# Layernorm pipelined over tiles, and the first scale block applied where the transposes leave PSUM

## The chip, the cores and the metric

The kernel runs on one core of one Trainium2 chip. The time is the device time of one execution in microseconds (us), given as a median of several executions. A core has these engines: PE (TensorE, matrix products), DVE (VectorE), ACT (ScalarE), POOL (GpSimd) and SP (SyncE, which here only issues transfers). PE reads SBUF, the large on-chip memory, and writes PSUM, a small one of eight banks, from which DVE or ACT must fetch the results. Each engine works through its own instructions in order.

## The reference

It is the attention half of a two-stream diffusion block: image tokens and text tokens are normalised and modulated by a conditioning vector `c`, projected, attend to each other jointly, and go through a gated output projection with a residual. B = 2, 256 image and 32 text tokens per batch element, D = 1152, all in bf16.

```python
mod_i = (silu(c) @ wmod_img).reshape(B, 6, 1, D)     # likewise mod_t with wmod_txt
shi, sci, gai = mod_i[:, 0], mod_i[:, 1], mod_i[:, 2]
hi = layernorm(x_img) * (1 + sci) + shi              # likewise ht
qkvi = hi @ wqkv_img                                 # likewise qkvt
q, k, v = concatenated text and image parts of qkvt, qkvi
p = softmax(q @ k.T * D ** -0.5)
a = p @ v
out_i = x_img + gai * (a_img @ wo_img)               # likewise out_t
```

## The kernel before, in words

The order of work is written out by hand: the pools are under a manual schedule, so every engine executes its instructions in the order of the program text, and waits between engines come from the data and from buffers.

The 512 image tokens are four tiles of 128 (`NIT` = 4, two for each batch element). D = 1152 is nine blocks of 128 (`KT` = 9). SP loads the tiles of x and then, block group by block group, the columns of the scale part of `wmod_img` (`w_sc_i`) and the matching rows of the V part of `wqkv_img` (`w_v_i`). The groups are `KC`, in the kernel before (0,2), (2,4), (4,6), (6,9). After them come the text tokens, the shift weights `w_sh_i`, the Q weights `w_q_i` in three pieces, and the other weights through six rotating buffers (`wpool`).

The image part begins like this:

- `silu_c` turns `c` to columns with a PE transpose and computes silu with an exponential on ACT (L124) and three DVE operations; the result is `sT`.
- `ln_stats` (L143 to L147) takes three `bn_stats` and one `bn_aggr` on DVE and the square root on ACT. `ln_apply` (L151, L152) takes the reciprocal and normalises on DVE.
- `x_transposes` (L161, L162) turns a normalised tile into nine 128x128 blocks, five in one PSUM buffer `tp` and four in another, and ACT copies them to `hT_i`.
- `mod_scale` (L169, L177, L179) computes 1 + scale for the blocks of one group: nine matmuls with a two-column right side for each block, and then one write to `mod_img`, on ACT or DVE.
- `apply_mod` (L187, L192, L196) multiplies blocks of `hT_i` by the scale in place, on DVE, POOL or ACT.
- `v_part` (L208) adds the blocks of one group to the V sums of one tile and one half of 512 columns. There are seven such sums (`va`), open from the first group to the last, and the buffers of PSUM for them and for `tp` are the seven of the pool `ps_mm`.

The program text interleaves these: while tiles 2 and 3 are normalised and transposed, the V matmuls of the second group run for tiles 0 and 1 already. When all groups are through, `v_rest` (L296) computes the last 128 columns of V, then come the shift (L308 to L312) and Q (L373). After that come K, the text stream, softmax, attention and the output projection (L560), which the change leaves alone.

Of the kernel before, what the change touches and what calls it, by code (L numbers as in the profile page):

```python
# [8 lines left out]
ACT = mybir.ActivationFunctionType  # L9
ALU = mybir.AluOpType  # L10
# [4 lines left out]
def kernel(  # L15
# [14 lines left out]
    nc = tc.nc  # L30
    bf = mybir.dt.bfloat16
    f32 = mybir.dt.float32
    PSUM = bass.MemoryType.PSUM

    B, NI, D = x_img.shape
    NT = x_txt.shape[1]
    P = 128
    KT = D // P
    NTOK = NI + NT
    NIT = (B * NI) // P  # L40
    TPB = NI // P
    NTT = B * NT
    CH = 384
    NCH = D // CH
# [1 line left out]
    SCALE = float(D) ** -0.5  # L46
    EPS = 1e-5

    KC = [(0, 2), (2, 4), (4, 6), (6, KT)]
    VW = 512  # L50
    NM = 1024

    const = ctx.enter_context(tc.tile_pool(name="const", bufs=1))
    wpool = ctx.enter_context(tc.tile_pool(name="w", bufs=6))
    act = ctx.enter_context(tc.tile_pool(name="act", bufs=1))
    work = ctx.enter_context(tc.tile_pool(name="work", bufs=2))
    small = ctx.enter_context(tc.tile_pool(name="small", bufs=4))
    ps_mm = ctx.enter_context(tc.tile_pool(name="ps_mm", bufs=7, space=PSUM))
# [11 lines left out]
    def w_view(src):  # L70
        return src.rearrange("(kt p) n -> p kt n", p=P)
# [10 lines left out]
    x_i = act.tile([P, NIT, D], bf)  # L82
    w_sc_i = wpool.tile([P, KT, D], bf, tag="w", name="w_sc_i")
    w_v_i = wpool.tile([P, KT, D], bf, tag="w", name="w_v_i")

    def load_x(i):
        nc.sync.dma_start(x_i[:, i, :], xi_t[:, i, :])

    def load_pair(ch):
        k0, k1 = KC[ch]  # L90
        nc.sync.dma_start(w_sc_i[:, :, k0 * P:k1 * P], w_view(wmod_img)[:, :, D + k0 * P:D + k1 * P])
        nc.sync.dma_start(w_v_i[:, k0:k1, :], w_view(wqkv_img)[:, k0:k1, 2 * D:3 * D])

    load_x(0)
    load_x(1)
    load_pair(0)
    load_x(2)
    load_x(3)
    for ch in range(1, len(KC)):
        load_pair(ch)  # L100
    x_t = act.tile([NTT, D], bf)
# [3 lines left out]
    w_q_i = load_w(wqkv_img, 0, K3)  # L105


    ident = const.tile([P, P], bf)
    make_identity(nc, ident[:])
    eps_t = const.tile([P, 1], f32)  # L110
# [10 lines left out]
    def silu_c():  # L121
        cT_ps = ps_sm.tile([P, B * KT], bf, tag="sm")
        nc.tensor.transpose(cT_ps[:], c18[:], ident[0:B * KT, 0:B * KT])
        nc.scalar.activation(e18[:], cT_ps[:], ACT.Exp, scale=-1.0)  # L124
        nc.vector.tensor_scalar_add(e18[:], e18[:], 1.0)
        nc.vector.reciprocal(e18[:], e18[:])
        nc.vector.tensor_mul(sT[:], cT_ps[:].rearrange("p (b kt) -> p kt b", b=B),
                             e18[:].rearrange("p (b kt) -> p kt b", b=B))
        nc.gpsimd.tensor_copy(sT32[:, :, 0:B], sT[:])
# [3 lines left out]
    def evac(out_ap, in_ap):  # L133
        if evac_idx[0] % 2 == 0:
            nc.vector.tensor_copy(out_ap, in_ap)  # L135
        else:
            nc.scalar.copy(out_ap, in_ap)  # L137
        evac_idx[0] += 1

    def ln_stats(x_ap, np_):  # L140
        stats = small.tile([P, NCH, 6], f32, tag="stats")
        for k in range(NCH):
            nc.vector.bn_stats(stats[0:np_, k, :], x_ap[:, k * CH:(k + 1) * CH])  # L143
        mv = small.tile([P, 2], f32, tag="mv")
        nc.vector.bn_aggr(mv[0:np_, :], stats[0:np_, :, :])
        rstd = small.tile([P, 1], f32, tag="rstd")
        nc.scalar.activation(rstd[0:np_, :], mv[0:np_, 1:2], ACT.Sqrt, bias=eps_t[0:np_, :])  # L147
        return mv, rstd

    def ln_apply(x_ap, np_, out_ap, mv, rstd):  # L150
        nc.vector.reciprocal(rstd[0:np_, :], rstd[0:np_, :])  # L151
        nc.vector.tensor_scalar(out_ap, x_ap, mv[0:np_, 0:1], rstd[0:np_, :], op0=ALU.subtract, op1=ALU.mult)  # L152

    xn_i = act.tile([P, NIT, D], bf, tag="A")
    hT_i = act.tile([P, KT, B * NI], bf, tag="Bt")

    def x_transposes(i):
        for (k0, k1) in ((0, 5), (5, KT)):
            tp = ps_mm.tile([P, 5, P], bf, tag="mm")
            for kt in range(k0, k1):  # L160
                nc.tensor.transpose(tp[:, kt - k0, :], xn_i[:, i, kt * P:(kt + 1) * P], ident[:])  # L161
            nc.scalar.copy(hT_i[:, k0:k1, i * P:(i + 1) * P], tp[:, 0:k1 - k0, :])  # L162

    mod_i = const.tile([P, 2 * KT, B], f32, name="mod_img")

    def mod_cols(wt, out_ps, j0, j1):
        for j in range(j0, j1):
# [4 lines left out]
    def mod_scale(ch, eng):  # L172
        k0, k1 = KC[ch]
        mps = ps_sm.tile([P, KT, B], f32, tag="sm")
        mod_cols(w_sc_i, mps, k0, k1)
        if eng == "dve":
            nc.vector.tensor_scalar_add(mod_i[:, KT + k0:KT + k1, :], mps[:, 0:k1 - k0, :], 1.0)  # L177
        else:
            nc.scalar.activation(mod_i[:, KT + k0:KT + k1, :], mps[:, 0:k1 - k0, :], ACT.Identity, bias=1.0)  # L179

    def apply_mod(kt, t0, t1, shift, eng):
        b = t0 // TPB
        sl = hT_i[:, kt, t0 * P:t1 * P]
        ap = mod_i[:, kt, b:b + 1] if shift else mod_i[:, KT + kt, b:b + 1]
        op = ALU.add if shift else ALU.mult
        if eng == 0:
            nc.vector.tensor_scalar(sl, sl, ap, None, op0=op)  # L187
        elif eng == 1:
            if shift:
                nc.gpsimd.tensor_scalar(sl, sl, 1.0, ap, op0=ALU.mult, op1=ALU.add)  # L190
            else:
                nc.gpsimd.tensor_scalar(sl, sl, ap, 0.0, op0=ALU.mult, op1=ALU.add)  # L192
        elif shift:
            nc.scalar.activation(sl, sl, ACT.Identity, bias=ap, scale=1.0)
        else:
            nc.scalar.activation(sl, sl, ACT.Identity, scale=ap)  # L196
# [5 lines left out]
    def v_part(i, half, ch):  # L202
        k0, k1 = KC[ch]
        if ch == 0:
            vacc[i, half] = ps_mm.tile([P, VW], f32, tag="mm", name=f"va{i}{half}")
        ps = vacc[i, half]
        for kt in range(k0, k1):
            nc.tensor.matmul(ps[:], lhsT=hT_i[:, kt, i * P:(i + 1) * P], rhs=w_v_i[:, kt, half * VW:(half + 1) * VW],  # L208
                             start=(kt == 0), stop=(kt == KT - 1))
        if k1 == KT:  # L210
            evac(v_i[:, i, half * VW:(half + 1) * VW], ps[:])


    silu_c()
    st = ln_stats(x_i[:, 0, :], P)
    ln_apply(x_i[:, 0, :], P, xn_i[:, 0, :], *st)
    x_transposes(0)
    st = ln_stats(x_i[:, 1, :], P)
    mod_scale(0, "act")
    ln_apply(x_i[:, 1, :], P, xn_i[:, 1, :], *st)  # L220
    for kt in range(*KC[0]):
        apply_mod(kt, 0, 1, False, 1)
    x_transposes(1)
    for half in range(2):
        v_part(0, half, 0)
    st = ln_stats(x_i[:, 2, :], P)
    for kt in range(*KC[0]):
        apply_mod(kt, 1, 2, False, 1)
    ln_apply(x_i[:, 2, :], P, xn_i[:, 2, :], *st)
    mod_scale(1, "act")  # L230
    for half in range(2):
        v_part(1, half, 0)
    for kt in range(*KC[1]):
        apply_mod(kt, 0, 2, False, 1)
    x_transposes(2)
    st = ln_stats(x_i[:, 3, :], P)
    for kt in range(*KC[0]):
        apply_mod(kt, 2, 3, False, 1)
    ln_apply(x_i[:, 3, :], P, xn_i[:, 3, :], *st)
    for i in range(2):  # L240
        for half in range(2):
            v_part(i, half, 1)
    x_transposes(3)
    for half in range(2):
        v_part(2, half, 0)
    for kt in range(*KC[0]):
        apply_mod(kt, 3, 4, False, 1)
    for kt in range(*KC[1]):
        apply_mod(kt, 2, 4, False, 0)
    mod_scale(2, "dve")  # L250
    for n, kt in enumerate(range(*KC[2])):
        apply_mod(kt, 0, 2, False, n % 2)
        apply_mod(kt, 2, 4, False, (n + 1) % 2)
    v_part(3, 0, 0)
    for half in range(2):
        v_part(2, half, 1)
    v_part(3, 0, 1)
    v_i = act.tile([P, NIT, D], bf, tag="A")
    SEVEN = [(i, half) for i in range(NIT) for half in range(2)][:7]
    for (i, half) in SEVEN[:4]:  # L260
        v_part(i, half, 2)
    mod_scale(3, "dve")
    for b in range(B):
        for n, kt in enumerate(range(*KC[3])):
            apply_mod(kt, b * TPB, (b + 1) * TPB, False, (n + b) % 3)
    for (i, half) in SEVEN[4:]:
        v_part(i, half, 2)
    for (i, half) in SEVEN:
        v_part(i, half, 3)


    xn_t = act.tile([NTT, D], bf)
    st_t = ln_stats(x_t[:, :], NTT)
    ln_apply(x_t[:, :], NTT, xn_t[:, :], *st_t)
    junk = small.tile([P, 1], f32, bufs=1)
    nc.scalar.activation(junk[:], eps_t[:], ACT.Exp)

# [129 lines left out]
    for blk, wq in enumerate([w_q_t, w_k_t]):  # L407
        for j0 in range(0, KT, FG):
            jn = min(FG, KT - j0)
            ps = ps_mm.tile([P, FG, NTT], f32, tag="mm")  # L410
            for j in range(j0, j0 + jn):
                for kt in range(KT):
                    nc.tensor.matmul(ps[:, j - j0, :], lhsT=wq[:, kt, j * P:(j + 1) * P], rhs=hT_t[:, kt, :],  # L413
                                     start=(kt == 0), stop=(kt == KT - 1))
# [212 lines left out]
```

## Time and profile before

| What | Value |
|---|---|
| median of 3 runs | 126.28 us (125.22 to 126.29) |
| profiled execution, its own time | 125.21 us |
| span of its instructions | 123.4 us |
| PE, DVE, ACT, POOL busy | 110.2, 54.0, 34.5, 25.2 us |
| transfers | 41.05 MB, mean 333 GB/s |
| granted TensorE clock | 0.998 |
| first scale matmul (L169) | 7.87 us after the span's start |
| transposes of tiles 0 to 3 (L161) start | 6.75, 9.79, 14.15, 16.87 us |
| first matmul of `v_rest` (L296) | 28.94 us |

The span runs from the first to the last instruction; the time of an execution holds some 2 us around it. Busy time is the union of an engine's instructions. "Idle before" and "<-" in rows of the profile name how long an engine stood before an instruction and what ended its wait. The chain of waits follows the work that ended last back from the end, so its rows add up to the span; the timeline merges neighbouring instructions of one form and gives start, length and count.

### The profile page before, as it was taken

The numbers are of one execution on the slowest core, as the hardware profiler recorded it, in microseconds if no ns is written. First come the engines' busy times: TensorE is split into PE (matmuls) and PEld (weight loads), VectorE is DVE, ScalarE is ACT, GpSimd is POOL, SyncE is SP. The second block draws the span as 40 slices with busy tenths as digits, with TensorE's granted clock in tenths as the row PEclk, the third lists the DMA queues.
The fourth block names the chain that finished last, engine by engine and source line by source line (L and its number), as shares of the span: only waits on it lengthen the run. The fifth ranks groups of instructions, "written<-read, shape, count | busy, mean of one in ns | idle before, by whom it ended". The sixth has DMA issues, their size and how long they took to land.

```text
span 123.4 us, 2694 instructions
## 1 busy us (share of the span) xinstructions
PE 110.2 (89%) x1137; PEld 66.8 (54%) x1137; DVE 54.0 (44%) x129; ACT 34.5 (28%) x85; POOL 25.2 (20%) x68
## 2 busy tenths in 40 slices
PE   0058989999999999999999999899969999999990
PEld 0044635546874445445444449767748766656660
DVE  0777633247690222202030621144275656646581
ACT  5444350231680301110031122143775500012000
POOL 4004334391064030304230000005260000000000
PEclk9999999999999999999999999999999999999999
DMA  3999999999999999999999999999999994220222
GB/s 107 270 365 377 376 383 319 353 415 408 415 403 407 403 411 409 412 409 406 406 377 384 404 414 413 404 412 406 408 403 420 373 410 190 90 96 0 101 80 64
DMA packets 22631, 41.05 MB, mean 333 GB/s; under 512 B 1179, under 2 KB 6459, under 8 KB 22619
## 3 DMA queue, kind: packets, MB, share of 16 engines
q1 hardware_dynamic: 21776, 39.74, 85.8%
q0 software_dynamic: 672, 1.06, 2.3%
q8 instruction: 9, 0.15, 0.5%
q10 hardware_dynamic: 171, 0.08, 0.2%
q14 instruction: 3, 0.02, 0.0%
HBM read 39.53 MB, written 1.35 MB: 331 GB/s over the span
## 4 chain that ended last, share of the span: by engine, by line
PE 82%; DVE 7%; ACT 5%; DMA 2%; issue 1%; ACTq 0%
PE qkps L373 29%; PE ps L560 13%; PE va L208 10%; PE aps L498 6%; PE gps L334 5%; PE ps L413 4%; PE sps L438 4%; PE mps L169 3%; ACT hT_i L162 2%; DMA x_i<-in_x_img_dram 2%; PE tp L161 2%; PE ps L579 2%; PE ps L296 2%; PE ps L303 2%; DVE v_t L135 1%; DVE xn_i L152 1%
## 5 line engine op out<-in xcount | busy, mean ns | idle before, releaser
L373 PE MATMUL qkps<-hT_i,t 128*128 128x512 bf16 x162 | 35.7, 379 | 0.0
L373 PEld LDWEIGHTS <-t 128*128 128x128 bf16 x162 | 15.5, 98 | 19.0 <-issue 0.7
L560 PE MATMUL ps<-t,aT 128*128 128x384 bf16 (+2 forms) x117 | 18.1, 314 | 0.0
L208 PE MATMUL va<-w_v_i,hT_i 128*128 128x512 bf16 x63 | 15.9, 401 | 0.1
L560 PEld LDWEIGHTS <-aT 128*128 128x128 bf16 x117 | 11.0, 98 | 6.8 <-issue 0.5
L563 DVE SCALAR_TENSOR_TENSOR tmp<-ps,rs,gb 128x384 bf16<-128x384 f32 (+2 forms) x13 | 7.6, 586 | 7.1 <-PE ps L560 7.1
L357 DVE TENSOR_SCALAR qkT<-qkps 128x512 bf16<-128x512 f32 x5 | 3.5, 692 | 15.4 <-PE qkps L373 15.4
L208 PEld LDWEIGHTS <-hT_i 128*128 128x128 bf16 x63 | 6.1, 102 | 6.9 <-issue 1.5
L192 POOL TENSOR_SCALAR hT_i<-hT_i,mod_img 128x128 bf16<-128x128 bf16 (+1 forms) x14 | 6.1, 450 | 14.5 <-ACT mod_img L179 6.5
L161 PE MATMUL tp<-ident,xn_i 128*128 128x128 bf16 x36 | 3.6, 265 | 5.7 <-DVE xn_i L152 5.7
L498 PE MATMUL aps<-pT,v_i 128*128 128x288 bf16 x36 | 6.7, 286 | 1.2 <-DVE rs L527 1.2
L344 POOL DMA_DIRECT2D mod_scratch<-g_sb x8 | 4.8, 600 | 12.9 <-DVE g_sb L338 6.1
L137 ACT CAST qkT<-qkps 128x512 bf16<-128x512 f32 x5 | 2.8, 586 | 16.0 <-PE qkps L373 16.0
L135 DVE CAST qkT<-qkps 128x512 bf16<-128x512 f32 x4 | 2.8, 688 | 8.4 <-PE qkps L373 8.4
L161 PEld LDWEIGHTS <-xn_i 128*128 128x128 bf16 x36 | 2.8, 120 | 6.6 <-DVE xn_i L152 6.4
L162 ACT COPY hT_i<-tp 128x640 bf16<-128x640 bf16 (+1 forms) x8 | 4.7, 642 | 5.9 <-PE tp L161 5.9
L143 DVE BATCH_NORM_STATS2 stats<-x_i 128x6 f32<-128x384 bf16 x12 | 5.9, 548 | 0.4 <-DMA x_i<-in_x_img_dram 0.4
L359 ACT ACTIVATE qkT<-qkps 128x512 bf16<-128x512 f32 x4 | 2.3, 596 | 11.4 <-PE qkps L373 11.4
L413 PE MATMUL ps<-hT_t,t 128*128 128x64 bf16 x162 | 5.0, 193 | 0.4 <-issue 0.4
L413 PEld LDWEIGHTS <-t 128*128 128x128 bf16 x162 | 4.9, 98 | 0.8 <-issue 0.5
L135 DVE CAST aT<-aps 128x288 bf16<-128x288 f32 x9 | 4.1, 458 | 2.5 <-PE aps L498 2.5
L498 PE MATMUL aps<-pT,v_t 128*128 128x288 bf16 x18 | 5.1, 286 | 0.0
(112 smaller groups left out, 128.9 us busy)
## 6 DMA issues: line engine op xcount, KB each, us to landing
t<-in_wmod_txt_dram SPq DMA_DIRECT2D x3, 2592.0 KB, 22.4
t<-in_wqkv_txt_dram SPq DMA_DIRECT2D x3, 2592.0 KB, 20.1
t<-in_wmod_img_dram SPq DMA_DIRECT2D x2, 2592.0 KB, 18.6
t<-in_wqkv_img_dram SPq DMA_DIRECT2D x6, 864.0 KB, 15.0
t<-in_wo_img_dram SPq DMA_DIRECT2D x1, 2592.0 KB, 22.3
t<-in_wo_txt_dram SPq DMA_DIRECT2D x1, 2592.0 KB, 24.3
w_sc_i<-in_wmod_img_dram SPq DMA_DIRECT2D x3, 576.0 KB, 7.6
w_v_i<-in_wqkv_img_dram SPq DMA_DIRECT2D x3, 576.0 KB, 7.9
```

Source lines behind the costliest of these rows:

```text
L135: nc.vector.tensor_copy(out_ap, in_ap)
L143: nc.vector.bn_stats(stats[0:np_, k, :], x_ap[:, k * CH:(k + 1) * CH])
L161: nc.tensor.transpose(tp[:, kt - k0, :], xn_i[:, i, kt * P:(kt + 1) * P], ident[:])
L162: nc.scalar.copy(hT_i[:, k0:k1, i * P:(i + 1) * P], tp[:, 0:k1 - k0, :])
L192: nc.gpsimd.tensor_scalar(sl, sl, ap, 0.0, op0=ALU.mult, op1=ALU.add)
L208: nc.tensor.matmul(ps[:], lhsT=hT_i[:, kt, i * P:(i + 1) * P], rhs=w_v_i[:, kt, half * VW:(half + 1) * VW], start=(kt == 0), stop=(kt == K ...
L334: nc.tensor.matmul(gps[32 * g:32 * g + 32, :], lhsT=lhs[:, kt, :], rhs=w_blk[:, kt, g * VC:(g + 1) * VC], start=(kt == 0), stop=(kt == KT ...
L373: nc.tensor.matmul(pss[j - j0][:], lhsT=wq[:, kt, j * P:(j + 1) * P], rhs=hT_i[:, kt, :], start=(kt == 0), stop=(kt == KT - 1))
L413: nc.tensor.matmul(ps[:, j - j0, :], lhsT=wq[:, kt, j * P:(j + 1) * P], rhs=hT_t[:, kt, :], start=(kt == 0), stop=(kt == KT - 1))
L498: nc.tensor.matmul(aps[:], lhsT=lhsT, rhs=pT[:, kj, :], start=(kj == 0), stop=(kj == 2))
L560: nc.tensor.matmul(ps[:, 0:cw], lhsT=aT[:, dt, t0:t0 + P], rhs=w_o_i[:, dt, cs], start=(dt == 0), stop=(dt == KT - 1))
L563: nc.vector.scalar_tensor_tensor(tmp[:, 0:cw], ps[:, 0:cw], rsum[(b, qi)][:], gb[:, b, cs], op0=ALU.mult, op1=ALU.mult)
```

## The change

The change touches only the part up to the last V group.

- `KC` becomes three groups of three blocks. SP loads x0, x1, the first scale group, x2, the first V group, x3, and then the pairs of the other two groups.
- A constant tile `junk_in` is set on DVE, and 13 matmuls of 128x512 on it (`keep_busy`) stand on PE: two ahead of the transposes of `c`, eleven behind. Their result is not used.
- Normalising is cut into steps (`Norm`). `norm_step(i)` takes the root of tile i, the first third of the statistics of tile i+1, applies tile i, and takes the other two thirds.
- `mod_scale(0)` comes ahead of everything of tile 0 but its statistics. `x_transposes(i)` moves the first three blocks into a PSUM buffer of their own, and three ACT activations with a per-partition scale write them to `hT_i`, already multiplied. The other six blocks go through a second buffer and one copy. The scaling of the first group by `apply_mod` is gone.
- After a tile's transposes come its V matmuls of the first group. The second and third group begin when all four tiles are through: `mod_scale` with its write on DVE, `apply_mod` shared over DVE, POOL and ACT for three blocks and both batch elements, then all V matmuls of the group.
- The text stream uses the same `Norm`.

```diff
-    KC = [(0, 2), (2, 4), (4, 6), (6, KT)]
+    KC = [(0, 3), (3, 6), (6, KT)]
...
-    load_pair(0)
+    nc.sync.dma_start(w_sc_i[:, :, 0:CH], w_view(wmod_img)[:, :, D:D + CH])
     load_x(2)
+    nc.sync.dma_start(w_v_i[:, 0:3, :], w_view(wqkv_img)[:, 0:3, 2 * D:3 * D])
     load_x(3)
...
+    junk_in = const.tile([P, VW], bf)
+    nc.vector.memset(junk_in[:], 1.0)
...
+    class Norm:
...
+        def part(self, k):
+            nc.vector.bn_stats(self.stats[0:self.n, k, :], self.x[:, k * CH:(k + 1) * CH])
+
+        def root(self):
+            nc.vector.bn_aggr(self.mv[0:self.n, :], self.stats[0:self.n, :, :])
+            nc.scalar.activation(self.rstd[0:self.n, :], self.mv[0:self.n, 1:2], ACT.Sqrt, bias=eps_t[0:self.n, :])
+
+        def apply(self):
+            nc.vector.reciprocal(self.rstd[0:self.n, :], self.rstd[0:self.n, :])
+            nc.vector.tensor_scalar(self.out, self.x, self.mv[0:self.n, 0:1], self.rstd[0:self.n, :],
+                                    op0=ALU.subtract, op1=ALU.mult)
...
     def x_transposes(i):
-        for (k0, k1) in ((0, 5), (5, KT)):
-            tp = ps_mm.tile([P, 5, P], bf, tag="mm")
-            for kt in range(k0, k1):
-                nc.tensor.transpose(tp[:, kt - k0, :], xn_i[:, i, kt * P:(kt + 1) * P], ident[:])
-            nc.scalar.copy(hT_i[:, k0:k1, i * P:(i + 1) * P], tp[:, 0:k1 - k0, :])
+        b = i // TPB
+        k1 = KC[0][1]
+        tp = ps_mm.tile([P, k1, P], bf, tag="mm", name="tpa")
+        for kt in range(k1):
+            nc.tensor.transpose(tp[:, kt, :], xn_i[:, i, kt * P:(kt + 1) * P], ident[:])
+        for kt in range(k1):
+            nc.scalar.activation(hT_i[:, kt, i * P:(i + 1) * P], tp[:, kt, :], ACT.Identity,
+                                 scale=mod_i[:, KT + kt, b:b + 1])
+        tp = ps_mm.tile([P, KT - k1, P], bf, tag="mm", name="tpb")
+        for kt in range(k1, KT):
+            nc.tensor.transpose(tp[:, kt - k1, :], xn_i[:, i, kt * P:(kt + 1) * P], ident[:])
+        nc.scalar.copy(hT_i[:, k1:KT, i * P:(i + 1) * P], tp[:])
...
+    warm = ps_mm.tile([P, VW], f32, tag="mm")
+    def keep_busy(n):
+        for _ in range(n):
+            nc.tensor.matmul(warm[:], lhsT=junk_in[:, 0:P], rhs=junk_in[:], start=True, stop=True)
+    keep_busy(2)
     silu_c()
+    keep_busy(11)
+    norms = [Norm(x_i[:, i, :], P, xn_i[:, i, :]) for i in range(NIT)]
+    for k in range(NCH):
+        norms[0].part(k)
+    def norm_step(i):
+        norms[i].root()
+        if i + 1 < NIT:
+            norms[i + 1].part(0)
+        norms[i].apply()
+        if i + 1 < NIT:
+            norms[i + 1].part(1)
+            norms[i + 1].part(2)
+    def v_tile(i, ch):
+        for half in range(2):
+            if (i, half) != (NIT - 1, 1):
+                v_part(i, half, ch)
+    mod_scale(0, "act")
+    norm_step(0)
     x_transposes(0)
+    v_tile(0, 0)
+    norm_step(1)
     x_transposes(1)
+    v_tile(1, 0)
+    norm_step(2)
     x_transposes(2)
+    v_tile(2, 0)
+    norm_step(3)
     x_transposes(3)
+    v_tile(3, 0)
     v_i = act.tile([P, NIT, D], bf, tag="A")
+    for ch in (1, 2):
+        mod_scale(ch, "dve")
+        for b in range(B):
+            for n, kt in enumerate(range(*KC[ch])):
+                apply_mod(kt, b * TPB, (b + 1) * TPB, False, (n + b) % 3)
+        for i in range(NIT):
+            v_tile(i, ch)
```

The removed hand-written order of tiles, scalings and V groups stands in the listing of the kernel before.

## The prediction

> **What bounds the kernel now.** I read the page first, then the chain of waits in order of time, then the timeline of the first 30 us, where the whole change lies. The page:
>
> ```profile
> span 123.4 us, 2694 instructions
> PE 110.2 (89%) x1137; PEld 66.8 (54%) x1137; DVE 54.0 (44%) x129; ACT 34.5 (28%) x85; POOL 25.2 (20%) x68
> PE 82%; DVE 7%; ACT 5%; DMA 2%; issue 1%; ACTq 0%
> ```
>
> PE is the bound, and the last line says that 18% of the chain is on others. The chain shows where (start, length, what):
>
> ```profile
> 7.50 1.18 ACT hT_i L162 x2
> 8.68 0.20 ACT rstd L147
> 8.90 0.17 DVE rstd L151
> 9.10 0.64 DVE xn_i L152
> 9.79 1.14 PE tp L161 x9
> 10.93 1.71 PE va L208 x4
> ...
> 16.87 0.47 PE tp L161 x5
> 17.34 0.02 issue
> 17.36 0.70 ACT hT_i L162
> 18.06 0.04 issue
> 18.10 0.59 PE va L208 x2
> ...
> 23.26 5.85 PE va L208 x27
> 29.11 1.00 PE ps L296 x18
> ```
>
> Two things are to be seen. The top six lines are a loop: ACT copies tile 0's transposes, only then takes tile 1's root, DVE normalises, PE transposes: tile 0's transposes began at 6.75, so 9.79 - 6.75 = 3.04 us from tile to tile. And at 17.34 to 18.10 PE stands until ACT has emptied a transpose buffer: the seven buffers of ps_mm are all taken. From 18.10 PE is unbroken to about 87 us, so what is lost or won before `v_rest` (L296, first matmul 28.94) shifts the end one for one.
>
> The timeline of the start (start, length, engine, line):
>
> ```profile
> 2.90 1.28 ACT L147 ACT_TABLE_LOAD   x1
> 5.58 0.29 ACT L147 ACTIVATE rstd<-mv,eps_t 128x1 f32<-128x1 f32 x1 [1.40 <-DVE mv L145]
> 7.87 0.56 PEld L169 LDWEIGHTS <-w_sc_i 128*128 128x128 bf16 x18 [0.25 <-DMA w_sc_i<-in_wmod_img_dram]
> 8.76 0.17 ACT L179 ACTIVATE mod_img<-mps 128x4 f32<-128x4 f32 x1
> 23.56 0.91 ACT L196 ACTIVATE hT_i<-hT_i,mod_img 128x256 bf16<-128x256 bf16 x2 [5.02 <-DVE mod_img L177]
> ```
>
> The root's table is loaded at 2.90 under idle time, the root runs at 5.58, and the first scale block, which a transfer releases at 7.87, holds back no normalising.
>
> **The change, part by part.**
>
> *Dummies.* 13 of 128x512. Cold rows (four L208 in 1.71 us) give 0.427 each, 5.6 in all; warm rows (16 in 3.48) 0.216, 2.8 in all. The constant's memset on DVE isn't in the trace: between 0.06 (eps_t, 128x1) and 0.69 (a 128x512 cast of DVE); I take 0.3, under DVE's idle time up to 2.91. Begun near 1.2 the dummies end between 4.5 and 7.5, while PE waits for the scale block anyway: cost 0. If the block came before them, the rest of them (up to 1 us) would be paid.
>
> *Transfers.* SP now sends x0, x1, 384 instead of 256 scale columns, x2, three blocks of V, x3. The scale slice grows from 576 to 864 KB. The extra 0.295 MB, at the 411 GB/s seen later, costs 0.7 us, at the 253 of 4 to 6 us 1.2. The windows of 6 to 10 us moved 326 and 386; I take 0.73, so the first scale matmul starts at 8.60 (ends of the range 8.5 and 9.1). x2, V and x3 follow, 2.0 MB more at about 370 GB/s to some 12.6, each ahead of its use below. Later loads keep their order in bytes.
>
> *What is queued on ACT.* `mod_scale(0)` now stands ahead of `norm_step(0)`. On ACT this puts the write of `mod_img` ahead of the first root, and so the first normalising of x waits for a weight transfer that it doesn't use. Behind that activation stand the table load, root 0, and through them DVE's apply and all transposes; on PE too tile 0's transposes stand behind the scale matmuls. The trace shows each load with the line of the activation that follows it; that the load isn't placed ahead of the `mod_img` write is my reading, worth between 0 and 1.28 us. I take 1.28, since L147's load is listed for the root's line. So: 27 scale matmuls 0.82 (the x27 row at 22.44) to 9.42; write 0.04 + 0.17 to 9.63; load 1.28 to 10.92; root 0.30 to 11.23; reciprocal 0.03 + 0.17; apply 0.03 + 0.58 to 12.05; transposes of tile 0 from 12.10. Now they start at 6.75.
>
> On this load the Trainium skill, "ScalarE: Activation LUTs", section "What ACT_TABLE_LOAD costs", speaks against the change more strongly: it adds a drain of about 1.38 us to each switch. The trace shows a root-side load of 1.28 and, for L124, its activation 10 ns behind the load. By the page the sum would be 1.4 us higher; I go by the row.
>
> *Eviction with the scale.* ACT's 128x128 scaled read isn't in the trace. Nearest rows: the scaled 128x256 (two in 0.91: start to start 0.41) and the root, 128x1 with a pointer (0.30 long, 0.20 start to start). Three of them cost 0.6 to 1.2; midway, 0.30 each, 0.9. The copy of six blocks: L162 takes 592 ns over four blocks and 692 over five, which gives 0.79 over six, of which 0.68 before the next may start. ACT per tile is 0.9 + 0.68 + 0.20 = 1.8 where it was 1.2. Removed in exchange: POOL's scalings of chunk 0 (L192, about 0.36 a block), which now delay the first V matmuls.
>
> *The period from tile to tile.* The root of tile i+1 is still written behind tile i's evictions on ACT. From the end of apply: 0.05 to PE, 0.35 until ACT reads, 0.9, 0.68, root 0.30, reciprocal 0.20, apply 0.61: 3.1 us. DVE's own work hides in it (three statistics 1.48, aggregate 0.24, reciprocal 0.17, apply 0.59 = 2.5). PE's work is 9 x 0.056 + 6 x 0.216 = 1.8, so PE idles 1.3 a tile: now it fills these gaps with V of chunk 1, and the new order has nothing there. Tile 3 is transposed from 12.1 + 3 x 3.1 = 21.4, now at 16.87.
>
> *Tile 3 and the seven buffers.* Six V sums are open then, so `tpa` has the last buffer; `tpb` waits for its three evictions, `va` for the copy of `tpb`. From 21.4: evictions done at 1.4, six transposes and copy to 2.8, three V matmuls to 3.5. With a free buffer it would be 1.5; the bounds of this wait are 0 and 2.0, and the row at 17.36 to 18.10 says that the waiting is real.
>
> *Chunks 1 and 2.* Each begins with 27 scale matmuls (0.85 to the last result) and then needs blocks that aren't scaled: write 0.20, first apply 0.32, and POOL's 0.57 for the second block (0.3 more on PE). Now `mod_scale` runs under V matmuls already released. Each chunk: 0.85 + 0.20 + 0.34 + 0.3 + 20 x 0.216 + 0.02 = 6.03, twice 12.05. `v_rest` starts at 21.4 + 3.5 + 12.05 = 36.95.
>
> *The sum.* 36.95 - 28.94 = 8.0 us later. What follows is the same PE work. Its weights land no later than now, but for those whose buffers come free up to 8 us later; the output weights among them land 8.7 us and more ahead of a use that is 8 us later too, so nothing is added. The profiled execution took 125.21 (span 123.4 and 1.8 around it): 133.2. It lies 1.07 under the median of 126.28; from the median it would be 134.3. I predict 133.8.
>
> *Clock.* Nine transposes take 1.14 us at 9.79 and 0.68 at 16.87, though the granted clock reads 1.00 in both: PE runs at half rate until about 13.5 us, after 3.7 us of unbroken work. The dummies give 3 to 6 us of work, so I expect full rate by 8.6. After them come some 2 us idle, 0.8 of scale work and 2.7 idle; no row shows whether that cools PE. Bounds: no loss; or half rate, where a tile's PE work of 9 x 0.107 + 6 x 0.427 = 3.5 exceeds the period by 0.4. I take no loss.
>
> The Trainium skill, "TensorE: Matmul & The Clock Gate", section "HAM oscillation — how this bites in real kernels", states that idle stretches beyond about 3.4 us bring the slow clock back. Neither stretch is so long alone; by it the sum stands, with half a microsecond to lose if both count as one.
>
> **Rivals.** *The load is hidden* or stands ahead of the `mod_img` write: 1.3 less; with a milder wait for buffers (1.3 less) 130.6. For it: the load waits for no data. Against: program order on ACT.
>
> *PE is cold in the tile stage*, so the dummies don't do what they are for: 0.4 on each of four tiles and half of 3.7 us while it warms up again: 133.2 + 3.5 = 136.7. For it: the two idle stretches. Against: PE is busy 60% of the time after.
>
> *Faster: PE alone sets the pace.* Warm from the first scale block on and fed without a gap, PE needs 81 x 0.025 + 36 x 0.056 + 63 x 0.216 = 17.6 us from 8.6: `v_rest` at 26.2, 2.7 earlier, of which the shift weights (landed at 29.51, needed at about 29.3 then) take 0.2: 122.7. It decides only if a tile's turn through ACT and DVE falls to 1.8 us and the first root isn't held at the scale block. Against it: DVE alone has 2.5 us a tile.
>
> **How the numbers follow.** Forecast 0.70, hidden load 0.12, cold PE 0.12, faster 0.04, and 0.02 for balance near zero. The range of 130.3 to 137.2 runs from the hidden load and mild buffer wait to the cold clock, and leaves out the faster case and the ends. A measurement of this kernel can tell about 1% (1.3 us) from no change; faster by more 0.04, within 0.03, slower 0.93.
>
> **What would show it.** Right: the table load just behind the `mod_img` write near 9.6; transposes of the tiles at about 12.1, 15.2, 18.3 and 21.4; PE waiting for ACT ahead of tile 3's second group of transposes; `v_rest` at about 37. Wrong: the first transposes before 10, tiles less than 2.5 apart, or `v_rest` before 29.

## The result, and the profile after

The changed kernel takes 135.26 us in the median of four runs (134.64 to 136.05), the kernel before 126.26 beside it: a ratio of 1.0753, with a 95% interval of 1.0701 to 1.0805. That is slower, as forecast, 1.5 us above the predicted 133.8 and inside the range. The profiled execution took 136.05 (span 134.3); it is the slowest of its four, and that of the kernel before (125.21) is the fastest of its own, so the profiled times put the loss at 10.8 us where the medians put it at 9.0. Ratios leave out executions that lie more than 1.5% above the fastest of their kernel; medians do not. The page of the changed kernel, with the clock as a row of its own this time:

```profile
span 134.3 us, 2709 instructions
...
PE 119.1 (89%) x1142; PEld 69.4 (52%) x1150; DVE 53.5 (40%) x128; ACT 36.9 (27%) x94; POOL 21.1 (16%) x58
...
PEclk9996589757999999999999999999999999999999
...
PE 77%; ACT 7%; DVE 6%; DMA 5%; issue 1%; POOL 1%; SPq 1%; ACTq 0%; POOLq 0%
```

The share of PE in the chain has fallen from 82% to 77%, and the granted clock, full in all 40 slices before, has two dents in the first quarter. `v_rest` starts at 40.28 us, where it started at 28.94: 11.34 later, slightly more than the 10.9 us by which the span grew. So the whole loss lies ahead of it.

The start in the timeline of the changed kernel (start, length, engine, line):

```profile
9.03 0.83 PE L184 MATMUL mps<-sT,w_sc_i 128*128 128x2 bf16 x27 [1.13 <-DMA w_sc_i<-in_wmod_img_dram]
...
9.90 0.17 ACT L194 ACTIVATE mod_img<-mps 128x6 f32<-128x6 f32 x1 [6.58 <-PE mps L184]
10.10 1.28 ACT L155 ACT_TABLE_LOAD   x1
...
11.39 0.29 ACT L155 ACTIVATE rstd<-mv,eps_t 128x1 f32<-128x1 f32 x1
...
12.55 0.50 PE L172 MATMUL tpa<-ident,xn_i 128*128 128x128 bf16 x3 [2.69 <-DVE xn_i L159]
```

ACT stands 6.58 us at the write of `mod_img`, which waits for a weight transfer; the table load and root 0 come only then. In the kernel before the same load ran at 2.90 and the same root at 5.58. The end of the tile stage:

```profile
22.32 0.34 PE L172 MATMUL tpa<-ident,xn_i 128*128 128x128 bf16 x3 [0.66 <-DVE xn_i L159]
...
23.63 0.49 PE L178 MATMUL tpb<-ident,xn_i 128*128 128x128 bf16 x6 [0.97 <-ACT hT_i L174]
...
25.02 1.44 PE L223 MATMUL va<-w_v_i,hT_i 128*128 128x512 bf16 x3 [0.89 <-ACT hT_i L179]
...
26.25 0.90 PE L184 MATMUL mps<-sT,w_sc_i 128*128 128x2 bf16 x27
...
34.21 0.82 PE L184 MATMUL mps<-sT,w_sc_i 128*128 128x2 bf16 x27
...
40.28 1.17 PE L308 MATMUL ps<-w_v_i,hT_i 128*128 128x128 bf16 x18
```

The second and third lines are waits for ACT's evictions, read here as waits for a PSUM buffer; e4 tests that reading. From 26.25 to 34.21 the second group takes 7.96 us, from 34.21 to 40.28 the third group, the same work, 6.07. The windows of the changed kernel, cut where the granted clock changes (columns: stretch, its length, busy time of PE, PEld, DVE, ACT, POOL, then the granted clock, DMA share and GB/s), show why:

```profile
4.38:7.80 3.42, 3.42 (x9) 0.93 (x7) 1.70 (x5) 0.00 (x0) 0.02 (x1) 1.00 0.96 301
7.80:11.21 3.41, 0.93 (x28) 0.74 (x27) 0.00 (x0) 1.29 (x2) 0.00 (x0) 1.00 1.04 395
11.21:14.62 3.41, 1.85 (x11) 1.34 (x13) 2.33 (x6) 1.93 (x7) 0.00 (x0) 0.50 1.08 392
14.62:18.04 3.42, 3.42 (x16) 1.73 (x15) 2.33 (x6) 1.66 (x6) 0.00 (x0) 0.50 1.07 385
18.04:21.45 3.41, 2.99 (x20) 1.24 (x18) 1.91 (x5) 2.16 (x7) 0.00 (x0) 1.00 1.07 341
21.45:24.86 3.41, 1.05 (x10) 0.60 (x10) 0.74 (x2) 1.58 (x5) 0.00 (x0) 1.00 1.04 359
24.86:28.28 3.42, 2.69 (x31) 1.52 (x32) 0.88 (x3) 0.94 (x3) 0.73 (x2) 0.50 1.05 408
28.28:31.69 3.41, 3.19 (x9) 1.21 (x9) 0.00 (x0) 0.07 (x1) 0.21 (x1) 0.50 1.04 411
```

The 1.00 of the first line doesn't mean full rate: no record stands for that stretch, and the dummies there follow each other in 0.427 us. Their work brings the full clock at 7.80, just when they end (the last starts at 7.27). PE works 0.93 us of the next 3.41, and the clock falls to 0.50 for two stretches. The same happens again after 21.45, where PE waits for tile 3 and its buffers.

### The profile page after: what moved, and what is told of

Its sections match the earlier page's. It is cut to its first block, busy times and chain, and to the rows that moved or that the text cites. A ratio compares the mean times of both kernels' runs of the same rounds, so it can differ in the third digit from the quotient of the medians.

```text
span 134.3 us, 2709 instructions
## 1 busy us (share of the span) xinstructions
PE 119.1 (89%) x1142; PEld 69.4 (52%) x1150; DVE 53.5 (40%) x128; ACT 36.9 (27%) x94; POOL 21.1 (16%) x58
## 4 chain that ended last, share of the span: by engine, by line
PE 77%; ACT 7%; DVE 6%; DMA 5%; issue 1%; POOL 1%; SPq 1%; ACTq 0%; POOLq 0%
PE qkps L385 26%; PE ps L572 12%; PE va L223 11%; DMA w_sc_i<-in_wmod_img_dram 5%; PE aps L510 5%; PE gps L346 5%; PE ps L425 4%; PE sps L450 3%; PE mps L184 3%; ACT hT_i L174 2%; PE ps L591 2%; ACT hT_i L179 2%; PE ps L308 2%; PE ps L315 1%; DVE v_t L138 1%
## 5 line engine op out<-in xcount | busy, mean ns | idle before, releaser
L385 PEld LDWEIGHTS <-t 128*128 128x128 bf16 x162 | 15.5, 98 | 19.0 <-issue 0.7
L223 PE MATMUL va<-w_v_i,hT_i 128*128 128x512 bf16 x60 | 18.6, 456 | 2.7 <-DVE hT_i L202 1.2
L223 PEld LDWEIGHTS <-hT_i 128*128 128x128 bf16 x63 | 6.8, 111 | 11.6 <-issue 4.5
L369 DVE TENSOR_SCALAR qkT<-qkps 128x512 bf16<-128x512 f32 x5 | 3.5, 691 | 15.5 <-PE qkps L385 15.5
L234 PE MATMUL warm<-junk_in 128*128 128x512 bf16 x13 | 5.9, 627 | 1.5 <-DVE eps_t L114 1.5
L207 POOL TENSOR_SCALAR hT_i<-hT_i,mod_img 128x256 bf16<-128x256 bf16 x4 | 2.0, 502 | 30.0 <-DVE mod_img L192 30.0
L346 PE MATMUL gps<-t,sT 128*32 128x288 bf16 x144 | 5.1, 287 | 0.0
L174 ACT ACTIVATE hT_i<-tpa,mod_img 128x128 bf16<-128x128 bf16 x12 | 3.5, 365 | 5.7 <-PE tpa L172 5.7
```

Of the source, the lines that this page charges most:

```text
L174: nc.scalar.activation(hT_i[:, kt, i * P:(i + 1) * P], tp[:, kt, :], ACT.Identity, scale=mod_i[:, KT + kt, b:b + 1])
L234: nc.tensor.matmul(warm[:], lhsT=junk_in[:, 0:P], rhs=junk_in[:], start=True, stop=True)
L346: nc.tensor.matmul(gps[32 * g:32 * g + 32, :], lhsT=lhs[:, kt, :], rhs=w_blk[:, kt, g * VC:(g + 1) * VC], start=(kt == 0), stop=(kt == KT ...
L385: nc.tensor.matmul(pss[j - j0][:], lhsT=wq[:, kt, j * P:(j + 1) * P], rhs=hT_i[:, kt, :], start=(kt == 0), stop=(kt == KT - 1))
```

## The experiments

All ratios are to the kernel before, run on the same chip. The starts of the first scale matmul and of `v_rest` are read from each profiled execution. The first follows the landing of the first scale weights, which differs by up to 1.1 us between runs that issue the same transfers, so this much of a difference in `v_rest` can come from there.

| Run | What differs | Median us | Ratio (95%) | First scale matmul us | `v_rest` us |
|---|---|---|---|---|---|
| changed kernel | | 135.26 | 1.0753 (1.0701 to 1.0805) | 9.03 | 40.28 |
| e1 | early root | 134.56 | 1.0724 (1.0641 to 1.0807) | 8.91 | 38.62 |
| e2 | no dummies | 135.59 | 1.0798 (1.0709 to 1.0887) | 8.46 | 38.33 |
| e3 | dummies in all gaps | 133.38 | 1.0626 (1.0543 to 1.0709) | 8.43 | 36.74 |
| e4 | half of tile 2 later | 133.99 | 1.0592 (1.0491 to 1.0693) | 8.61 | 39.23 |
| e5 | groups interleaved | 128.73 | 1.0256 (1.0186 to 1.0326) | 9.50 | 32.84 |
| e6 | e5 and early root | 127.21 | 1.0149 (1.0089 to 1.0209) | 9.33 | 31.26 |
| e10 | e6 and dummies in the gaps | 125.23 | 0.9953 (0.9921 to 0.9984) | 9.03 | 29.49 |
| e7 | before, with early dummies | 125.48 | 0.9994 (0.9947 to 1.0041) | 7.60 | 29.87 |
| e8 | before, scale ahead of root | 129.29 | 1.0302 (1.0241 to 1.0364) | 7.05 | 32.84 |
| e9 | before, dummies also in the gaps | 125.01 | 0.9952 (0.9910 to 0.9994) | 8.14 | 28.84 |

**e1: the early root.**

```diff
+    norms[0].root()
     mod_scale(0, "act")
     norm_step(0)          # takes no root for i == 0 now
```

> The changed kernel with one line moved: the square root of tile 0 is written ahead of the first scale block's mod_img write on ACT, so the table load and root 0 run before the scale weights land. Theory (the queue on ACT holds the first tile): tile 0's transposes start at about 9.9 us instead of 12.55, the start of v_rest and the end come 1.6 to 2.9 us earlier, so about 132.4 to 133.7. Rival (the first V weights, landed at 11.89, or the period of the tiles take over at once): transposes near 9.9 all the same, but v_rest and the end within 0.7 us of the changed kernel's 135.3.

The timeline of e1:

```profile
3.17 1.28 ACT L155 ACT_TABLE_LOAD   x1
...
5.56 0.29 ACT L155 ACTIVATE rstd<-mv,eps_t 128x1 f32<-128x1 f32 x1 [1.11 <-DVE mv L154]
...
9.61 0.33 PE L172 MATMUL tpa<-ident,xn_i 128*128 128x128 bf16 x3
...
11.83 2.72 PE L223 MATMUL va<-w_v_i,hT_i 128*128 128x512 bf16 x6 [1.33 <-ACT rstd L155]
...
14.34 0.53 PE L172 MATMUL tpa<-ident,xn_i 128*128 128x128 bf16 x3
```

The transposes come 2.94 us earlier. Then PE waits until 11.83. The profile names ACT's root there, but the V matmul doesn't read it; its weights landed at 11.79. Tile 1 is 1.77 earlier, `v_rest` 1.66. The median gained only 0.7 us and its interval covers the changed kernel, so by the time alone this run is inconclusive. The pairs e5 and e6, and e8, decide the question.

**e2: no dummies.**

```diff
-    junk_in = const.tile([P, VW], bf)
-    nc.vector.memset(junk_in[:], 1.0)
...
-    keep_busy(2)
     silu_c()
-    keep_busy(11)
```

> The changed kernel without the constant tile and the 13 dummy matmuls. Theory (the full clock that they bring is granted from 7.8 us to 11.2 us, when PE stands, and is gone when the transposes begin): within 0.6 us of the changed kernel, 134.7 to 135.9. Rival (the dummies do bring the later work forward): slower by 1 us or more, 136.3 or above.

135.59 against 135.26, with wide intervals: no gain from the dummies can be seen, as the theory said. The clock behaves differently all the same: the profiled execution, the fastest of the four at 134.47, had the full clock from 15.5 to 25.8 and from 29.2 on, so it lost it for one stretch where the changed kernel lost it for four.

**e3: PE kept at work.**

```diff
-    keep_busy(11)
+    keep_busy(15)
...
     mod_scale(0, "act")
+    fill(8)               # the same dummies, into the small PSUM tile
...
     v_tile(0, 0)
+    fill(4)               # likewise after tiles 1 and 2, and twice in tile 3
...
         mod_scale(ch, "dve")
+        fill(2)
```

> The changed kernel with more dummies: 4 more at first, 8 behind the first scale matmuls, 4 behind each of the tiles 0 to 2, 4 between the two groups of transposes of tile 3 and 4 behind them, and 2 behind the scale matmuls of each later group, so that PE has no idle stretch over 1 us before v_rest. Theory (about 3 us of the loss is the clock, which falls to half from 11.2 to 18.0 and from 24.9 to 31.7 us): the granted clock stays at 1.00 from about 8 us on, v_rest starts near 37.5 instead of 40.3, and the end is 2 to 3.5 us earlier, 131.8 to 133.3. Rival (the clock costs little because ACT sets the pace of the tiles): clock full but the end within 1 us of 135.3.

The windows of e3 over the stretches after which the changed kernel lost its clock:

```profile
7.60:11.00 3.40, 3.14 (x39) 1.79 (x38) 0.00 (x0) 1.68 (x3) 0.00 (x0) 1.00 1.05 395
...
21.20:24.60 3.40, 3.32 (x26) 1.68 (x25) 0.00 (x0) 1.68 (x4) 0.00 (x0) 1.00 1.04 400
```

The first scale matmul, the first transposes of the four tiles and `v_rest` in the timeline of e3:

```profile
8.43 0.82 PE L188 MATMUL mps<-sT,w_sc_i 128*128 128x2 bf16 x27
...
11.94 0.34 PE L172 MATMUL tpa<-ident,xn_i 128*128 128x128 bf16 x3 [0.54 <-DVE xn_i L159]
...
15.06 0.33 PE L172 MATMUL tpa<-ident,xn_i 128*128 128x128 bf16 x3
...
18.11 0.33 PE L172 MATMUL tpa<-ident,xn_i 128*128 128x128 bf16 x3
...
21.15 0.33 PE L172 MATMUL tpa<-ident,xn_i 128*128 128x128 bf16 x3
...
36.74 1.17 PE L322 MATMUL ps<-w_v_i,hT_i 128*128 128x128 bf16 x18
```

The clock is 1.00 from 7.6 us to the end, and `v_rest` starts 3.54 us earlier although PE executes 36 dummies more. Not all of that is the clock: the first scale matmul began 0.60 earlier, and from it to `v_rest` it is 28.31 us instead of 31.25, 2.94 less. The median falls by 1.9 us, just short of the 2 to 3.5 expected. The profiles show more than the medians, since the changed kernel's is its slowest of four and that of e3 its fastest (132.51); two of e3's four, at 133.8 and 134.0, have a mean granted clock of 0.983 and so did not keep it throughout.

**e4: a buffer freed for tile 3.**

```diff
-    v_tile(2, 0)
+    v_part(2, 0, 0)
     norm_step(3)
     x_transposes(3)
+    v_part(2, 1, 0)
     v_tile(3, 0)
```

> The changed kernel with the second V half of tile 2 in the first group written behind the transposes of tile 3, so that a PSUM buffer is free for their second group. Theory (PE's stand at 22.9 to 25.0 us is the wait for buffers): the 1.0 us wait ahead of the second transposes goes, the scale matmuls of the second group start 1.0 to 2.0 us earlier, and with the shorter idle stretch perhaps the second fall of the clock; the end at 131.5 to 134.3. Rival (the same stand comes back at the next buffer or at the copy): within 0.6 us of 135.3.

The four executions are of two kinds: 132.77 and 132.99 at a mean granted clock of 0.973 and 0.974, and 135.0 and 135.5 at 0.948 and 0.946. The median of 133.99 lies between them, the ratio in the table rests on the first two alone, and the profile is that of the 135.0. Its timeline:

```profile
21.91 0.34 PE L172 MATMUL tpa<-ident,xn_i 128*128 128x128 bf16 x3 [1.30 <-DVE xn_i L159]
...
22.09 0.50 PE L178 MATMUL tpb<-ident,xn_i 128*128 128x128 bf16 x6
...
23.22 2.21 PE L223 MATMUL va<-w_v_i,hT_i 128*128 128x512 bf16 x6 [0.64 <-ACT hT_i L174]
...
25.23 0.90 PE L184 MATMUL mps<-sT,w_sc_i 128*128 128x2 bf16 x27
```

The wait ahead of the second transposes is gone, and the scale matmuls follow tile 3's transposes after 3.32 us instead of 3.93. Of the 1.0 to 2.0 expected that is 0.6: a wait of 0.64 stands at the next buffer, as the rival has it, and the clock fell to half at 23.8 here too. In the two faster executions the mean clock is near the 0.969 of e5's profile, where it fell once, and not near the 0.948 of two falls; that the freed buffer spared them the second fall is thus likely, but no profile of them shows it.

**e5: the interleaving put back.**

```diff
     norm_step(2)
+    mod_scale(1, "act")
+    for kt in range(*KC[1]):
+        apply_mod(kt, 0, 2, False, 1)
     x_transposes(2)
-    v_tile(2, 0)
+    v_part(2, 0, 0)
+    v_tile(0, 1)
     norm_step(3)
     x_transposes(3)
+    v_tile(1, 1)
+    v_part(2, 1, 0)
     v_tile(3, 0)
+    for n, kt in enumerate(range(*KC[1])):
+        apply_mod(kt, 2, 4, False, n % 3)
+    mod_scale(2, "dve")
...
+    v_tile(2, 1)
+    v_tile(3, 1)
...
+    for i in range(NIT):
+        v_tile(i, 2)
```

> The changed kernel with the interleaving of groups put back: the scale matmuls of the second group stand ahead of tile 2's transposes, POOL scales that group's blocks for tiles 0 and 1, their V matmuls of the second group run around tile 3's transposes, the second V half of tile 2 stands behind tile 3's transposes, and the third group's scale matmuls stand ahead of the last V matmuls of the second. Theory (the largest part of the loss is that PE has no V work of the second group in the tiles' gaps): v_rest starts at 33.8 to 36 instead of 40.3, the end is 4.3 to 6.5 us earlier, 128.8 to 131. Rival (the late first tile and the clock are the larger part, so the gaps only move): within 2.5 us of 135.3.

The timeline of e5 from tile 3 on:

```profile
22.59 0.34 PE L172 MATMUL tpa<-ident,xn_i 128*128 128x128 bf16 x3
...
22.76 0.50 PE L178 MATMUL tpb<-ident,xn_i 128*128 128x128 bf16 x6
...
23.10 2.75 PE L223 MATMUL va<-w_v_i,hT_i 128*128 128x512 bf16 x12
...
25.69 0.82 PE L184 MATMUL mps<-sT,w_sc_i 128*128 128x2 bf16 x27
...
26.59 6.42 PE L223 MATMUL va<-w_v_i,hT_i 128*128 128x512 bf16 x29
...
32.84 1.17 PE L317 MATMUL ps<-w_v_i,hT_i 128*128 128x128 bf16 x18
```

Tile 3 is no earlier than in the changed kernel (22.59 against 22.32), but no row names a wait, and `v_rest` follows after 10.25 us instead of 17.96. The median falls by 6.5 us, as much as was expected at most, and `v_rest` comes 1 us earlier than the 33.8 expected at best. The run also freed the buffer of e4, and the clock stayed full from 16.5 on, so these 6.5 us hold three things: the interleaving, the buffer, and the second fall of the clock. Against the two faster executions of e4 (132.9 in the mean), which have the buffer and, by their mean clock, one fall, e5 is 4.1 us lower: an estimate of the interleaving alone.

**e6: the early root on top of e5.**

```diff
+    norms[0].root()
     mod_scale(0, "act")
     norm_step(0)          # takes no root for i == 0 now
```

> The kernel of the run before with root 0 written ahead of the first scale block's write on ACT as well. Theory (both losses add, and the first V weights at 11.8 take over part of the second): 1.0 to 1.8 us below the run with the interleaving alone, 127.3 to 129.8. Rival (the interleaved V work already hides the first tile's delay): within 0.5 us of it.

127.21, 1.5 us below e5, and `v_rest` 1.58 earlier, both as the theory has it; the intervals of the two ratios overlap a little.

**e7: the kernel before with the dummies alone.**

```diff
+    keep_busy(2)
     silu_c()
+    keep_busy(8)
     st = ln_stats(x_i[:, 0, :], P)
```

> The kernel before with the constant tile and 10 dummy matmuls alone (2 ahead of the transposes of c, 8 behind). Theory (the full clock comes at 7 to 8 us instead of 13.7 and stays, but PE then waits for the second scale block, landed at 12.4, and for the tiles): 0 to 0.7 us faster than the kernel before. Rival (the half clock up to 13.7 us is paid in full): 1.2 to 2 us faster; or the dummies delay the first transposes: slower by 0.5 or more.

0.9994 of the kernel before, so no effect, which is the low end of the theory, but not for its reason. The windows of e7:

```profile
3.20:6.60 3.40, 3.12 (x8) 0.82 (x6) 2.90 (x10) 1.42 (x2) 0.20 (x1) 1.00 0.99 273
6.60:10.00 3.40, 1.76 (x36) 1.50 (x37) 2.72 (x8) 1.50 (x4) 0.92 (x2) 1.00 1.05 381
10.00:13.40 3.40, 2.92 (x27) 1.24 (x26) 2.97 (x8) 1.65 (x4) 0.99 (x3) 0.51 1.10 372
```

The full clock came at 6.6 and was lost at 10.0, and it returned only at 16.9, later than the 13.7 of the kernel before. This execution, at 126.26, is one of the slower of its ten.

**e8: the kernel before with the queue of the change.**

```diff
     silu_c()
+    mod_scale(0, "act")
     st = ln_stats(x_i[:, 0, :], P)
...
-    mod_scale(0, "act")   # between tile 1's statistics and its apply
```

> The kernel before with one line moved: the scale matmuls of the first group and their write on ACT stand ahead of tile 0's statistics and root. Theory (the queue on ACT makes root 0 wait for the scale weights and the table load): the transposes of tile 0 start near 11.1 us instead of 6.75, the table load at about 8.8, and the end is 2.0 to 3.5 us later than the kernel before. Rival (the first tile has slack, since PE has no V weights before 9.2 us): within 1 us of the kernel before.

The timeline of e8:

```profile
7.72 0.17 ACT L179 ACTIVATE mod_img<-mps 128x4 f32<-128x4 f32 x1 [4.50 <-PE mps L169]
...
7.92 1.28 ACT L147 ACT_TABLE_LOAD   x1
9.21 0.29 ACT L147 ACTIVATE rstd<-mv,eps_t 128x1 f32<-128x1 f32 x1
...
10.38 1.14 PE L161 MATMUL tp<-ident,xn_i 128*128 128x128 bf16 x9 [2.69 <-DVE xn_i L152]
...
32.84 1.17 PE L296 MATMUL ps<-w_v_i,hT_i 128*128 128x128 bf16 x18
```

One line moved in an otherwise unchanged kernel costs 3.0%: tile 0 is 3.63 us later, `v_rest` 3.90, and the median 3.6 us higher than the 125.71 beside it, just above the 3.5 expected at most. The scale block landed earlier here (7.00) than assumed, which is why the transposes stand at 10.4 and not at 11.1. The move also puts tile 0's transposes behind the scale matmuls on PE, but their row names DVE as what they wait for, so the time is lost on ACT. The rival, slack ahead of the first tile, is out.

**e9: the kernel before with the clock kept**, beside the dummies of e7.

```diff
     mod_scale(0, "act")
+    fill(4)
...
+    fill(5)
     mod_scale(1, "act")
```

> The kernel before with the 10 early dummies and dummies in the stretches in which PE waits after them: 4 behind the first scale matmuls and 5 ahead of the second. Theory (the early dummies brought nothing since the full clock was lost again from 10.0 to 16.9 us; kept, it lets the V matmuls of the first tiles end earlier): clock 1.00 from about 7 us on, tile 2's transposes at 13.4 to 13.9 instead of 14.15, the end 0.4 to 1.2 us earlier than the kernel before. Rival (transfers and the tiles' turn set the pace up to 17 us): clock kept, but within 0.3 us of the kernel before.

In the profiled execution the clock is 1.00 from 7.3 us on. The median time is 0.5% lower, with the interval just short of 1, but it mixes two kinds: six of the twelve executions have a mean granted clock of 1.000 and took 124.0 to 124.5, below all 23 of the kernel before beside them (124.7 to 127.0); the other six have 0.986 and took 125.5 to 126.2. So the theory's gain is there in the half of the executions whose mean clock is full. The profile, of the first kind, doesn't show where it comes from: tile 2's transposes start at 14.05 and `v_rest` at 28.84, where they were at 14.15 and 28.94, as the rival has it, PE still waiting for the second scale block, which landed at 12.68. The span is 0.7 us shorter, so most of the difference lies behind `v_rest`, and its cause stays open.

**e10: interleaving, early root and a kept clock**, on top of e6.

```diff
-    keep_busy(11)
+    keep_busy(15)
...
     x_transposes(0)
+    fill(6)
     v_tile(0, 0)
```

> The run with the interleaving and the early root, with 4 more early dummies and 6 behind tile 0's transposes, while PE waits for the first V weights. Theory (the half clock from 9.0 to 15.9 us is what is left beside the larger first transfer): clock 1.00 throughout, tile 1's transposes near 13.7 instead of 14.8, the end 1.0 to 1.5 us below that run's 127.2, that is 125.7 to 126.2 and level with the kernel before. Rival (the V weights and the turn of the tiles set the pace): within 0.5 us of 127.2.

In e6 the first V matmul stood at 12.28. The timeline of e10:

```profile
11.92 1.46 PE L223 MATMUL va<-w_v_i,hT_i 128*128 128x512 bf16 x6 [0.24 <-ACT rstd L155]
...
13.21 0.33 PE L172 MATMUL tpa<-ident,xn_i 128*128 128x128 bf16 x3
...
22.34 0.82 PE L184 MATMUL mps<-sT,w_sc_i 128*128 128x2 bf16 x27
...
29.49 1.17 PE L325 MATMUL ps<-w_v_i,hT_i 128*128 128x128 bf16 x18
```

125.23 us, 2.0 below e6, more than expected, and 0.5% below the kernel before (0.9921 to 0.9984). Tile 1's transposes start at 13.21, 1.58 earlier than in e6, and the clock is 1.00 from 5.6 us on. `v_rest` is 1.77 earlier than in e6. Of these, 0.36 need not be the clock's: the first V matmuls begin at 11.92 and not 12.28, as their weights landed at 11.88 and not 12.24. With e9 this is the best of the versions; the two can't be told apart.

## Why the prediction was right, and where it was off

**The causes** were named rightly. With `mod_scale(0)` first, root 0 waits on ACT for weights. Write, load, root, reciprocal and apply took 0.17, 1.28, 0.29, 0.16 and 0.58, as summed. The table load wasn't hidden, so the first rival is out, and the root followed it by 0.01 us, so the row gave its price. e8 shows the same loss in the other kernel. That the new order has no V work of another group for PE's gaps, and that the later groups begin with blocks that aren't scaled, is what e5 takes back: 6.5 us, together with the buffer and the second fall of the clock.

**The sum at full clock** was right. It put `v_rest` 28.35 us behind the first scale matmul (36.95 - 8.60); in e3, the changed kernel with its clock kept, it is 28.31. Its terms: tile to tile 3.1 predicted, 3.12, 3.05 and 3.04 in e3; in the changed kernel three scaled evictions 0.9 and 0.88 (an activation every 0.25 us rather than 0.30); the six-block copy 0.79 and 0.81; second transposes 1.4 behind the first, measured 1.31; third group 6.03 and 6.07. The constant's memset took 0.48, not 0.3, and delayed nothing that counts. Two figures don't come out of their rows: 0.295 MB at the 326 and 386 GB/s that the prediction names take 0.90 and 0.76 us, not 0.73, and x2, V and x3 are 1.5 MB, not 2.0; with 1.5 the 12.6 us come out, and the V weights landed at 11.89.

**The step that failed** is "I take no loss" for the clock. 40.28 is 3.33 us past the sum. Of this, the scale block accounts for 0.43 (9.03 instead of 8.60); tile 0 to tile 1 at half clock took 3.56 instead of 3.1, 0.46; the three V matmuls of tile 3 came 0.43 late (3.93 after its transposes, not 3.5); the second group took 7.96 instead of 6.03, 1.93. The last three, 2.8 us, are the clock's price in this execution; e3 puts it at 2.94 from the first scale matmul on, and at 1.9 in the median. The rival "PE is cold" was the true one in kind. It priced one loss in the tile stage, 3.5 us; in fact the clock fell twice, and the second fall, in the dense V matmuls of the second group, cost most. The measured 135.26 lies as near to that rival's 136.7 as to the forecast's 133.8, so the number alone wouldn't have told the two apart. That the forecast came within 1.5 us is in part luck: what the clock takes differs between executions, and the profiled one lies 2.9 us past the 133.2 that the sum gives for it.

The Trainium skill, "TensorE: Matmul & The Clock Gate", section "HAM oscillation — how this bites in real kernels", gives the rule of no idle gaps of PE beyond about 3.4 us, which the prediction held against each single stretch. The measurement decides against reading it so: the waits around the first fall were 1.13 and 2.69 us, with scale matmuls between them, and the clock was lost. The same page's section "What's actually happening" speaks of a free-running window of 3413 ns; that fits, as the windows above change at multiples of 3.41 us.

**Where the 11.34 us went.** Taken back in the order of the runs, from 40.28: interleaving, with the buffer and the second fall of the clock, 7.44 (e5; counted from tile 0's transposes it is 7.94, as they came 0.50 later there); the root behind the scale block 1.58 (e6); the rest of the clock, with 0.36 of earlier V weights, 1.77 (e10). What is left is 0.55, and no run takes it apart; the larger first transfer, the tiles' turn and the scaled evictions, which no run undoes, may all have a part in it. The parts depend on the order: the root alone took 3.90 from the kernel before (e8), and gave 1.66 in e1, where the V weights at 11.79 took over.

**The transfer.** 8.60 was predicted, with 9.1 as the far end; runs with the same first transfers began their scale matmuls between 8.43 and 9.50. What makes the difference of 1.07 us stays open.

## What to carry to other kernels

Ahead of moving an instruction up in a hand-written order, look at what it waits for and at everything behind it in its engine's queue: one small write that waits for a weight transfer held a table load, a root and all transposes, and cost 3%. Where tiles are pipelined strictly one after another, compare each tile's turn with PE's work on it: here the turn was 3.0 us and the work 1.8, an estimate from the rows' rates, and the V work of another group in the gap was the larger part (4.1 us, estimated) of the largest single gain (6.5 us). Dummy matmuls at the start brought nothing here in the medians (e2, e7); the clock that they raise has to be held through the gaps (e3, e10).

## What the runs showed of the hardware

The full clock was lost without any idle stretch of 3.4 us: after stretches of 3.4 us in which PE was busy 0.93 and 1.05 (changed kernel), 1.76 (e7) and 1.96 (e2), while it was kept after 2.24 (e2) and after 2.67 and more (e3). A stretch with 1.95 kept it in e10, so the busy time of the profile alone doesn't give the limit. Nor does it for raising the clock: a stretch with 2.92 of 3.40 wasn't enough in e7, and one with 2.88 was in e2 (25.8 to 29.2 us). Where an execution gains the clock and loses it shifts from run to run: the first full stretch began between 5.6 and 7.8 us in the kernels with early dummies. Matmuls on a constant of 1.0 raise the clock: without them it came at 13.7 (kernel before), 15.5 (e2) and 17.9 (e8).
